# Forty-eight drains on TensorE between the loop and the tail of a decode kernel

## The chip, the core and the metric

The kernel runs on one core of a Trainium2 chip. Five engines of the core work side by side, each on its own stream of instructions: TensorE (PE in the profile, its weight loads PEld), VectorE (DVE), ScalarE (ACT), GpSimd (POOL) and SyncE (SP). They meet only at semaphores. Loads from the chip's main memory are issued here by SyncE and done by 16 DMA engines. An engine's sequencer reads the stream and hands products and vector operations on to the engine; drains, register steps and branches it does itself. The metric is the device time of one execution in microseconds (us); a profiled execution gives the trace and a page that sums it up.

## What is computed

One decode step of a block with attention and a gated feed-forward part side by side: batch 4, one token, width 512; 32 query heads over 8 key and value heads of 128; a window of the last 4096 of 16384 cached keys.

```python
xn = _layernorm(x, axis=-1)
return x + _A_ref(xn, ...) + _B_ref(xn, ...)

def _A_ref(x, k_cache, v_cache, wq, wo):
    q = (x @ wq)                                   # 32 heads of 128
    k = k_cache[:, :, Sk - W:, :]; v = v_cache[:, :, Sk - W:, :]
    scores = einsum("bhqd,bhkd->bhqk", q, k) * (Dh ** -0.5)
    p = softmax(scores, axis=-1)
    return einsum("bhqk,bhkd->bhqd", p, v) @ wo

def _B_ref(x, w_gate, w_up, w_down):
    return (silu(x @ w_gate) * (x @ w_up)) @ w_down
```

## The kernel before

The keys and values of 4 batches and 8 heads are cut into 16 pieces, each with one head of two batches, 2 MB of keys and 2 MB of values. Both are double-buffered in SBUF (`KB`, `VB`). SyncE issues all loads in one hand-written order: the query weights, two pieces of keys, the gate and up weights, then keys and values in turn, at last the down weights, the values of the last piece in two halves and the output weights `WO` in four cuts (chunks 0 to 15, 16 to 25, 26 to 29, 30 and 31 of 32). A load of keys waits until TensorE has transposed the keys that lay in its buffer (L216), a load of values until the products with the old values are done (`s_pv`, L220); the last values wait for the sixteenth of these (L241), the `WO` cuts behind them on the queue for nothing of their own.

TensorE runs a loop of 8 passes (L425) with two pieces in each. For a piece it transposes the keys (L382) into PSUM, from where VectorE copies them to SBUF (L294), forms the scores (`scores`, L385), and one piece later the products with the values (`pv`, L405). The maxima for the softmax go around by VectorE: it takes the row maxima of the scores (`row_max`, L299), TensorE transposes them (`max_rows`, L396, L398), VectorE reduces them to one value for each of 8 rows and makes a small diagonal of them (L304 to L306), TensorE subtracts that from all scores by one product (`shift`, L400), and ScalarE takes the exponential (L263). Helper `mm` (L353, recorded as L354) issues all products but the transposes.

Behind the loop stands a tail without a loop, in this order on TensorE: `max_rows` of the last piece (L439), the second half of the products with the values of the last but one (L440), the last `shift` (L441), the products with the gate and the up weights (L443 to L449), the input for the residual (L451), the products with the last values (L452 to L454), with the down weights (L457), four transposes of the attention's result (L462), a product that sorts the heads (L468), and 64 output products with `WO` (L472 to L476), which wait at chunks 0, 16, 26 and 30 for the four cuts. VectorE has in the tail the last maxima, normalisations of the attention's result (`norm`, L308), the gate, two copies of the sorted result (`OB` L345, `OP` L347) and the copy of the sum to SBUF (L349), from where two transfers of 2 KB take it out.

Everything on an engine runs in the order in which it is written; there is no planner.

Of the kernel before, what the change touches and what calls it, by code (L numbers as in the profile page):

```python
# [10 lines left out]
def bass_parallel_sum__sliding_block_cached__swiglu_ffn__decode_kernel(  # L11
# [10 lines left out]
    out: bass.AP,  # L22
):
    B, _, D = A_x.shape
    _, HKV, Sk, Dh = A_k_cache.shape
    HQ = A_wq.shape[1] // Dh
    F = B_w_gate.shape[1]
# [143 lines left out]
    with nc.Block() as block:  # L171
# [180 lines left out]
        def _(eng):  # L352
            def mm(o, l, r, start=False, stop=True):  # L353
                return eng.matmul(o, l, r, start=start, stop=stop, skip_group_check=True)  # L354
# [18 lines left out]
            def mask(bank):  # L373
                return mm(ps_S[bank][:].rearrange("p (t c) -> p t c", c=C), mkr[:],
                          mkc[:].rearrange("j (o c) -> j o c", o=1).to_broadcast([2, NT, C]), start=True)

            def transposes(s, ev, b):
                for g in range(NG):
                    eng.wait_ge(s_ev, ev + g + 1)
                    for k in range(8):  # L380
                        a = b * KVN + s * HKN + 128 * (8 * g + k)
                        last = eng.transpose(kt_ps[g][:, k, :], KB[:, a:a + 128], ident[:])  # L382
                    last.then_inc(s_tr, 1)

            def scores(s, ev, b, q):  # L385
                if s == 0:
                    mask(b)
                eng.wait_ge(s_ev, ev + 2 * NG)
                for t in range(HT):
                    o = C * (s * HT + t)  # L390
                    n = min(WIDE, SN - o)
                    last = mm(ps_S[b][:, o:o + n], KT[:, s * HKN + 128 * t:s * HKN + 128 * (t + 1)], q(n))
                if s == 1:
                    last.then_inc(s_sc, 1)

            def max_rows(n):  # L396
                eng.wait_ge(s_rm, n)
                mm(mt_ps, RM[:], ident[:], start=True).then_inc(s_mt, 1)  # L398

            def shift(bank, n):  # L400
                eng.wait_ge(s_dg, n)
                mm(ps_S[bank][:].rearrange("p (t c) -> p t c", c=C), ones[0:C, :],
                   Dg[:].rearrange("j (o c) -> j o c", o=1).to_broadcast([C, NT, C])).then_inc(s_sh, 1)

            def pv(bank, s, n):  # L405
                p = bank * PS
                if s == 0:
                    eng.wait_ge(d_v[bank], n[0])
                    eng.wait_ge(s_p, n[1])
                    eng.wait_ge(s_nrm, n[1])  # L410
                    for j in range(SN // 128):
                        mm(den_ps, ones[:], P[:, p + 128 * j:p + 128 * (j + 1)], start=(j == 0))
                for t in range(HT):
                    a = bank * KVN + s * HKN + 128 * t
                    o = p + C * (s * HT + t)
                    last = mm(O_wide, VB[:, a:a + 128], P[:, o:o + WIDE], start=(s == 0 and t == 0))
                if s == 1:
                    last.then_inc(s_pv, 1)
# [6 lines left out]
            with eng.Fori(0, ND // 2) as r:  # L425
                for b in range(2):
                    n = 2 * r + (b + 1)
                    ev = 4 * NG * r + 2 * NG * b
                    q = lambda w, b=b: QF[:, ds(r * (2 * WIDE) + b * WIDE, w)]
                    eng.wait_ge(d_k[b], r * 16 + 16)  # L430
                    transposes(0, ev, b)
                    max_rows(n)
                    pv(b, 1, n)
                    scores(0, ev, b, q)
                    shift(1 - b, n)
                    transposes(1, ev + NG, b)
                    pv(1 - b, 0, (r * 16 + 16, n))
                    scores(1, ev + NG, b, q)
            max_rows(ND + 1)  # L439
            pv(0, 1, ND + 1)  # L440
            shift(1, ND + 1)  # L441
# [64 lines left out]
```

## Time and profile before

| | us |
|---|---|
| median of 3 runs | 197.38 |
| lowest and highest run | 197.1, 198.93 |
| the profiled execution, its time | 196.99 |
| the profiled execution, its span | 195.2 |
| VectorE busy, share of the span | 59% |
| TensorE busy, share of the span | 82% |

The span goes from the first to the last recorded instruction; what lies around it, 1.8 us in the profiled execution, is start and end of the program. A line of the timeline has the start in us, the duration, the engine, the line of the kernel, the operation, the tile written and those read, and how many neighbours were merged; brackets hold the idle time ahead of it and who ended it. Engine names with a q (PEldq, SPq) are that engine's sequencer. The DMA engines are busy nearly all the way:

```profile
GB/s 216 430 430 433 435 423 428 425 433 433 430 437 430 430 433 430 430 437 430 433 430 433 430 430 433 430 430 430 430 433 430 430 430 433 430 431 417 442 404 64
```

Each number is the rate in one of 40 equal slices of the span.

### The profile page before, as it was taken

To read this page: it belongs to the slowest core of one execution; us is meant where nothing else is said; L and a number is where in the kernel's file an instruction comes from. 1 tells how busy PE (TensorE), PEld (TensorE's weight loads), DVE (VectorE), ACT (ScalarE), POOL (GpSimd) and SP (SyncE) were. 2 spreads that over 40 slices of the span, in tenths; PEclk is the share of its full clock that TensorE was granted. 3 is DMA by queue.
4 is the path that set the end of the run, shared out by engine and by line. 5 is a ranking of instruction groups with operands and counts; after the bars stand their busy time and mean duration, and the time that the engine had idled before them with its cause. 6 is when DMAs were issued, how large, how long until landed. Compare 5 with 4: busy or idle time off the path is not lost.

```text
span 195.2 us, 7741 instructions
## 1 busy us (share of the span) xinstructions
PE 160.9 (82%) x3458; PEld 139.5 (71%) x3458; DVE 114.8 (59%) x250; ACT 16.6 (9%) x26; POOL 10.3 (5%) x23
## 2 busy tenths in 40 slices
PE   0127999379898989898989898989898989898954
PEld 0113898368887888788878887878787878786742
DVE  1004777337676767676767676767676767675610
ACT  6600101001010101010101010101010101010100
POOL 8930000000000000000000000000000000000000
PEclk9999999879999999999999999999999999999999
DMA  6999999999999999999999999999999999999991
GB/s 216 430 430 433 435 423 428 425 433 433 430 437 430 430 433 430 430 437 430 433 430 433 430 430 433 430 430 430 430 433 430 430 430 433 430 431 417 442 404 64
DMA packets 5934, 81.10 MB, mean 416 GB/s; under 512 B 668, under 2 KB 680, under 8 KB 936
## 3 DMA queue, kind: packets, MB, share of 16 engines
q1 hardware_dynamic: 5912, 81.01, 97.5%
q8 instruction: 5, 0.08, 0.1%
q10 hardware_dynamic: 16, 0.01, 0.0%
q14 instruction: 1, 0.01, 0.0%
HBM read 81.01 MB, written 0.00 MB: 415 GB/s over the span
## 4 chain that ended last, share of the span: by engine, by line
DMA 63%; PE 32%; issue 1%; DVE 1%; SPq 1%; DVEq 0%
DMA kbuf<-in_A_k_cache_dram 48%; PE ps_kt L382 16%; DMA wo_sb<-in_A_wo_dram 9%; PE ps_s L354 8%; DMA wq_sb<-in_A_wq_dram 6%; PE ps_o L354 5%; PE ps_kt L354 2%; PE ps_acc L354 2%; DVE kT L294 1%; SPq L225 1%; DVE kT L282 0%; SPq L229 0%; DVE y_sb L349 0%; DVE qz L285 0%; DVEq L293 0%
## 5 line engine op out<-in xcount | busy, mean ns | idle before, releaser
L294 DVE COPY kT<-ps_kt 128x1024 bf16<-128x1024 bf16 x128 | 79.5, 684 | 25.3 <-PE ps_kt L382 25.3
L382 PE MATMUL ps_kt<-ident,kbuf 128*128 128x128 bf16 x1024 | 62.8, 219 | 10.6 <-DMA kbuf<-in_A_k_cache_dram 10.6
L382 PEld LDWEIGHTS ps_kt<-ident,kbuf 128*128 128x128 bf16 x1024 | 57.3, 98 | 15.8 <-issue 15.7
L354 PE MATMUL ps_o<-p,vbuf 128*128 128x64 bf16 x1120 | 39.0, 194 | 0.0
L354 PEld LDWEIGHTS ps_s<-qz,kT 128*128 128x128 bf16 x1024 | 32.1, 99 | 6.7 <-issue 3.6
L354 PEld LDWEIGHTS ps_o<-p,vbuf 128*128 128x128 bf16 x1120 | 35.8, 99 | 1.1
L354 PE MATMUL ps_s<-qz,kT 128*128 x1024 | 35.3, 193 | 1.2
L299 DVE TENSOR_REDUCE rm<-ps_s 128x8 bf16<-128x512 f32 x17 | 11.8, 692 | 23.5 <-PE ps_s L354 23.5
L263 ACT ACTIVATE p<-ps_s 128x512 bf16<-128x512 f32 x17 | 10.1, 597 | 162.4 <-PE ps_s L354 162.4
L354 PE MATMUL ps_o<-p,ones 128*128 128x128 bf16 (+1 forms) x69 | 6.9, 220 | 4.4 <-DMA vbuf<-in_A_v_cache_dram 3.0
L354 PEld LDWEIGHTS ps_o<-p,ones 128*128 128x128 bf16 x69 | 4.5, 98 | 5.5 <-DMA vbuf<-in_A_v_cache_dram 3.2
L354 PE MATMUL ps_kt<-wq_sb,xnT 128*32 128x512 bf16 x32 | 3.6, 629 | 5.6 <-DMA wq_sb<-in_A_wq_dram 5.6
L354 PE MATMUL ps_s<-dg,ones 8*128 8x512 bf16 x17 | 6.5, 385 | 0.0
L354 PE MATMUL ps_s<-mkc,mkr 2*128 2x512 bf16 x17 | 6.5, 385 | 0.0
L359 PE MATMUL ps_acc<-i,xn 4*128 4x4 f32 x4 | 0.6, 254 | 7.1 <-ACT xn L260 7.1
L354 PEld LDWEIGHTS ps_kt<-wq_sb,xnT 128*32 128x32 bf16 x32 | 1.2, 137 | 7.2 <-issue 7.2
L282 DVE STREAM_TRANSPOSE kT<-ps_kt 128x512 f32<-128x512 f32 x2 | 1.4, 716 | 8.3 <-PE ps_kt L354 8.3
L354 PE MATMUL ps_acc<-wo_sb,oP 128*4 128x256 bf16 x64 | 4.1, 272 | 1.8 <-DMA wo_sb<-in_A_wo_dram 1.8
L359 PEld LDWEIGHTS ps_acc<-i,xn 4*128 4x128 f32 x4 | 0.6, 207 | 7.1 <-issue 7.1
L310 DVE TENSOR_REDUCE den<-ps_o 128x8 f32<-128x128 f32 x18 | 4.9, 274 | 1.0 <-PE ps_o L354 1.0
L207 POOL MEMSET vbuf<- 128x6144 f32 x1 | 5.2, 5222 | 0.0
L354 PEld LDWEIGHTS ps_acc<-wo_sb,oP 128*4 128x4 bf16 x64 | 2.5, 84 | 3.3 <-DMA wo_sb<-in_A_wo_dram 1.9
(65 smaller groups left out, 48.0 us busy)
## 6 DMA issues: line engine op xcount, KB each, us to landing
kbuf<-in_A_k_cache_dram SPq DMA_DIRECT2D x16, 2048.0 KB, 12.6
vbuf<-in_A_v_cache_dram SPq DMA_DIRECT2D x15, 2048.0 KB, 11.3
wq_sb<-in_A_wq_dram SPq DMA_DIRECT2D x1, 4096.0 KB, 12.4
vbuf<-in_A_v_cache_dram SPq DMA_DIRECT2D x2, 1024.0 KB, 9.2
wo_sb<-in_A_wo_dram SPq DMA_DIRECT2D x1, 2048.0 KB, 14.4
wg_sb<-in_B_w_gate_dram SPq DMA_DIRECT2D x1, 1792.0 KB, 25.8
wu_sb<-in_B_w_up_dram SPq DMA_DIRECT2D x1, 1792.0 KB, 29.4
wd_sb<-in_B_w_down_dram SPq DMA_DIRECT2D x1, 1792.0 KB, 15.0
```

What stands on the lines that cost most here:

```text
L207: eng.memset(VB[:, HKN:].bitcast(FP32), 0.0)
L225: eng.dma_start(VB[:, a:a + HKN], kv_ap(A_v_cache, d)[:, :, h * HKN:(h + 1) * HKN]).then_inc(done, 16)
L263: eng.activation(P[:, d % 2 * PS:d % 2 * PS + SN], ps_S[d % 2][:], ACT.Exp, scale=SCALE).then_inc(s_p, 1)
L282: eng.transpose(qT[:, 512 * n:512 * n + 512], ps_kt[n][:])
L294: eng.tensor_copy(KT[:, u * HKN + 1024 * g:u * HKN + 1024 * (g + 1)], kt_ps[g].rearrange("p a b -> p (a b)")).then_inc(s_ev, 1)
L299: eng.tensor_reduce(RM[:], ps_S[bank][:].rearrange("p (t c) -> p c t", c=C), AX.X, ALU.max).then_inc(s_rm, 1)
L310: eng.tensor_reduce(den[:], den_ps.rearrange("p (t c) -> p c t", c=C), AX.X, ALU.add)
L354: return eng.matmul(o, l, r, start=start, stop=stop, skip_group_check=True)
L359: last = eng.transpose(xT_ps[:, c * B:(c + 1) * B], xn[:].rearrange("b (p c) -> b c p", c=NC)[:, c, :], I4[:])
L382: last = eng.transpose(kt_ps[g][:, k, :], KB[:, a:a + 128], ident[:])
```

## The change

Behind the loop and ahead of `max_rows(ND + 1)` TensorE gets 48 drain instructions. A drain is an instruction of the sequencer: it goes on when the engine's own work before it is done. They carry no semaphore, neither a wait nor a step. Nothing else differs; on the other four engines the programs are the same.

```diff
                     pv(1 - b, 0, (r * 16 + 16, n))
                     scores(1, ev + NG, b, q)
+
+            for _ in range(48):
+                eng.drain()
             max_rows(ND + 1)
             pv(0, 1, ND + 1)
             shift(1, ND + 1)
```

## The prediction

> **What bounds the kernel now.** I read the page's summary first, then the chain of waits in order of time, then the timeline behind the loop, and last single sequencer rows and stretches of the granted clock. The page's span and the last steps of the chain:
>
> ```profile
> span 195.2 us, 7741 instructions
> DMA 63%; PE 32%; issue 1%; DVE 1%; SPq 1%; DVEq 0%
> ...
> 170.88 1.05 PE ps_o L354 x32
> 171.95 0.54 SPq L225
> ...
> 173.83 16.82 DMA wo_sb<-in_A_wo_dram
> 190.64 0.04 issue
> 190.69 2.23 PE ps_acc L354 x32
> 192.92 0.03 issue
> 192.95 0.43 DVE y_sb L349
> ```
>
> The chain leaves TensorE at 171.95 us, inside the last pass of the loop, when the product that frees a V buffer lets SyncE issue its last loads. From there to 190.64 it is transfers. TensorE returns only for the second half of the output product, whose weights have just landed. So everything that TensorE does between 172 and 190 us, and the place of the change with it, lies beside the chain. The question is by how much. The timeline of that stretch (start, duration; in brackets the idle time before it and who ended it):
>
> ```profile
> 173.18 2.02 SPq L229 DMA_DIRECT2D wo_sb<-in_A_wo_dram  x4
> ...
> 176.73 1.06 PE L354 MATMUL ps_s<-qz,kT 128*128 x32
> 177.83 0.69 DVE L299 TENSOR_REDUCE rm<-ps_s 128x8 bf16<-128x512 f32 x1 [1.15 <-PE ps_s L354]
> ...
> 178.57 0.22 PE L354 MATMUL ps_acc<-ident,rm 128*8 128x128 bf16 x1 [0.78 <-DVE rm L299]
> ...
> 178.72 1.11 PE L354 MATMUL ps_o<-p,vbuf 128*128 128x64 bf16 x32
> ...
> 179.76 0.39 PE L354 MATMUL ps_s<-dg,ones 8*128 8x512 bf16 x1
> ...
> 180.08 0.94 PE L354 MATMUL ps_kt<-wg_sb,xnT 128*32 128x448 bf16 x16
> ...
> 182.17 2.03 PE L354 MATMUL ps_o<-p,vbuf 128*128 128x64 bf16 x64
> ...
> 184.13 1.69 PE L354 MATMUL ps_acc<-wd_sb,guT 128*4 128x256 bf16 x28
> ...
> 186.08 0.41 DVE L345 COPY oB<-ps_kt 32x512 bf16<-32x512 bf16 x1 [1.03 <-PE ps_kt L462]
> 186.54 0.22 PEld L354 LDWEIGHTS ps_kt<-oB,rep 32*128 32x128 bf16 x4 [0.68 <-DVE oB L345]
> ...
> 186.98 0.44 DVE L347 CAST oP<-ps_kt 128x128 bf16<-128x128 f32 x1 [0.49 <-PE ps_kt L354]
> 187.65 1.65 PEld L354 LDWEIGHTS ps_acc<-wo_sb,oP 128*4 128x4 bf16 x32 [0.89 <-DVE oP L347]
> 187.68 1.91 PE L354 MATMUL ps_acc<-wo_sb,oP 128*4 128x256 bf16 x32 [0.74 <-DMA wo_sb<-in_A_wo_dram]
> ...
> 192.52 0.09 PEld L354 LDWEIGHTS ps_acc<-wo_sb,oP 128*4 128x4 bf16 x4 [0.28 <-DMA wo_sb<-in_A_wo_dram]
> ```
>
> Three things are to be seen. TensorE stands idle for 0.78 us just where the drains go, waiting for VectorE's row maxima. From 178.57 on its products follow one another without a wait on a transfer, and the two hand-overs to VectorE at 186 us depend on them: a delay at 178.57 passes whole to 187.42, where `OP` is ready (186.98 + 0.44). At the output product it meets the slack. A hand-over from VectorE took 0.05 (186.08 + 0.41 to 186.54), so TensorE could have begun near 187.47 and began at 187.65, on a transfer: 0.18 us. The 32 products took 1.91, of which the last one's own time is some 0.27; that is (1.91 − 0.27)/31 = 0.053 each. Sixty of them would be done with at 187.68 + 60 × 0.053 = 190.86, and the last four begin at 192.52 on a transfer: 1.66 us. Together a delay of about **1.8 us is free**; beyond it each microsecond shows.
>
> **The change, step by step.** It removes and moves nothing. It adds 48 instructions for TensorE's sequencer. Behind them on TensorE stand the transposing product of L398 and all of the tail; VectorE's `shift` waits for that product and ScalarE's last exponential for the shift. SyncE is not held: its four `WO` issues begin at 173.18 and take 2.02, and nothing behind the loop frees a buffer for it. So no transfer moves, and with the last weights at 192.52 the end can't come earlier: a gain is excluded but for scatter.
>
> *The first drain* waits for the last score product. What that costs, and what a drain takes when nothing runs:
>
> ```profile
> L491 PEldq DRAIN  x1: 8/8/8, 0.3 to 0.3; - x1
> L171 PEldq DRAIN  x1: 432/432/432, 192.5 to 192.5; - x1
> L425 PEldq ALU_OP  x1: 32/32/32, 177.2 to 177.2; - x1
> L425 PEldq COMPARE_BRANCH  x1: 76/76/76, 177.3 to 177.3; - x1
> ```
>
> The drain at the kernel's end began at 192.5 and took 432 ns, to about 192.95, where the last product had ended (192.92 in the chain). So a drain waits for TensorE to run empty, and adds little more. The last scores end at 176.73 + 1.06 = 177.79; VectorE starts on them at 177.83. I let the first drain end at 177.84, and it costs nothing by itself.
>
> *The other 47* find TensorE empty. The drain at the start took 8 ns. What the sequencer needs between two of its own instructions has to come from others: the counter step and the branch of L425 stand next to each other in the program. Asked for in stretches of 10 ns, the first begins in 177.16 to 177.17 and the second in 177.26 to 177.27, so 98 ns apart with some 5 ns either way. Of these the first executes 32, and 66 pass between. A drain then costs about 8 + 64 = 72 ns, an estimate from these rows. The bounds: not under 8 ns, execution alone; not much over 98 ns, the whole distance, if a drain costs the sequencer what the counter step does. I take 72, since both parts are rows of TensorE's own sequencer. 47 × 0.072 = 3.38, so the last ends at 177.84 + 3.38 = 181.22, and the product begins with a hand-over of 0.03 (192.92 to 192.95) at 181.25 in place of 178.57: **a delay of 2.7 us**, less the slack of 1.8: 0.9 us at the end. The bounds by the same sum: 8 ns gives 47 × 0.008 = 0.38, done before the maxima are, and nothing; 98 ns gives 4.61, a delay of 3.9 and 2.1 at the end.
>
> The Trainium skill, "VectorE: DVE Perf Modes", section "The DRAIN you can't avoid", speaks of boilerplate drains of about 12 ns on all engines; by that the whole row would be 48 × 12 ns = 0.58 us, under the idle 0.78, and the change free. Its "Perfetto Trace Analysis", section "Sequencer-only Instruction (DRAIN, etc)", says that such a record holds execution alone, fetch and decode lying ahead of it; the 66 ns above agree.
>
> *The clock.* The drains leave TensorE without a product from 177.79 to 181.25, 3.46 us. What an idle stretch did to the clock, by stretches as long as the one at half clock (PE busy, PEld, DVE, ACT, POOL, granted clock, DMA), and what the half clock did to two groups:
>
> ```profile
> 34.55:37.96 3.41, 0.46 (x12) 0.46 (x13) 1.10 (x2) 0.00 (x0) 0.00 (x0) 1.00 1.01 425
> 37.96:41.37 3.41, 3.03 (x62) 2.94 (x58) 0.34 (x1) 0.00 (x0) 0.00 (x0) 0.50 0.99 418
> 184.73:188.14 3.41, 2.16 (x38) 1.58 (x36) 1.09 (x4) 0.00 (x0) 0.00 (x0) 1.00 0.97 414
> 191.56:194.97 3.41, 1.34 (x20) 0.44 (x14) 0.43 (x1) 0.00 (x0) 0.00 (x0) 1.00 0.04 13
> ...
> 194.97:195.17 0.20, 0.00 (x0) 0.00 (x0) 0.00 (x0) 0.00 (x0) 0.00 (x0) 0.51 0.00 0
> ...
> 37.50 0.40 PE L354 MATMUL ps_o<-p,ones 128*128 128x128 bf16 x4 [3.03 <-DMA vbuf<-in_A_v_cache_dram]
> 37.73 1.71 PE L354 MATMUL ps_o<-p,vbuf 128*128 128x64 bf16 x32
> ```
>
> An idle time of 3.03 us left one stretch of 3.41 with 0.46 us of product, and the next ran at half clock. So did what followed the stretch with 1.34. The one with 2.16 did not do it. With stretches of that length laid over an idle 3.46 us at any phase, one of the two that share it holds at least 1.73 of idle, so at most 1.68 of product; in four of five phases it holds 1.34 or less. The half clock is then likely, and its stretch lies 2.1 to 3.4 us deep in the products that follow. The 32 products of 64 columns took 1.71 against 1.11: at that ratio 3.41 us at half clock do the work of 2.2, and 1.2 are lost; products that wait for the columns alone would lose half, 1.7. With 2.1 us so lost at the least ratio it is 0.7. I take **1.3 us**, all beyond the slack, since the 1.8 is used up.
>
> The sum: 2.7 − 1.8 + 1.3 = **2.2 us**. The profiled execution took 196.99 beside its span of 195.2, which makes 199.2; the median of the three runs was 197.38 (197.1 to 198.93), which makes 199.6. I put it between, at 199.4, from a base of 197.2.
>
> **The rivals.** *The clock stays.* The drains cost 72 ns, the delay is 2.7, and 0.9 shows: 198.1. For it: a stretch between 1.34 and 2.16 of product is not in the trace, and one phase in five falls there. Against: both low stretches were followed by the half clock. The Trainium skill, "TensorE: Matmul & The Clock Gate", Part 1, wants at least one idle window of about 3.4 us before the clock drops, in windows that run free of the kernel; by it the gap of 3.46 would almost never hold a whole one, and the result would be this 198.1. The stretch with 0.46 us of product speaks against that rule here.
>
> *The drains are cheap, and it is not slower.* The place is the wait for the maxima and the slack at the output product; the price is the drain's, and it decides at (1.8 + 178.57 − 0.03 − 177.84)/47 = 0.053 us. Under 53 ns a drain, nothing shows but what the clock adds; at 16 ns they end within the idle 0.78. For it: the record of 8 ns. Against: the 66 ns between two neighbours on the same sequencer. Time: 197.2.
>
> *The drains are dearer.* At 98 ns each the delay is 3.9, of which 2.1 show, and with the clock's 1.4 it is 3.5: 200.7. A fetch of the longer program would fall here too. The queue of instructions is this row of the page:
>
> ```profile
> q8 instruction: 5, 0.08, 0.1%
> ```
>
> 0.1% of 16 × 195.2 us is 3.1 us for five, 0.6 each at most if one were exposed. Against it: no row of the sequencer but the branch shows more than 98 ns.
>
> That the change doesn't do what it says: drains could be dropped when the program is built. The built program has the 48 in a row ahead of the product, so I give this nothing beyond the cheap case.
>
> **How the numbers follow.** Cheap 0.20, clock stays 0.13, forecast 0.52, dearer 0.15. The forecast's own range is 198.7 (clock at 0.7, a base of 197.0) to 200.2. For 8 in 10 the range reaches down to the cheap case, as its price is an end of the unknown cost, and up to the dearer one: 197.0 to 201.0. A change of under 1%, 1.97 us, can't be told from none here. The forecast of 2.2 lies just past it: some seven tenths of its chance fall beyond, 0.36, the dearer case nearly whole, 0.15, and a little of the second, 0.01: slower 0.52. Faster 0.01 for scatter, the rest, 0.47, within.
>
> **What would show it.** In the changed profile: 48 drains on TensorE's sequencer, the first ending near 177.8 us, the others about 72 ns apart with 8 ns of execution; the transposing product near 181.2 with an idle time of about 3.4; half the granted clock in a stretch of 3.41 us that begins between 179.9 and 182.7; `WO` issued at 173.2 and landed as before; the wait ahead of the last four output products gone. The chain of waits should then run over TensorE's tail and not over `WO`. Wrong it would be if the drains stood much closer or wider, if the clock stayed whole, or if the chain still ended on the `WO` transfer.

## The result and the profile after

The changed kernel took 200.02 us, the median of 6 runs (199.47 to 200.67), against 197.29 of 6 runs before: a ratio of 1.0121 with a 95% interval of 1.0083 to 1.016, so 1.6 to 3.2 us slower, 2.4 at the middle. The profiled execution took 199.47 with a span of 197.7, 2.5 us more than the one before. It was the shortest of the six.

The rows of the new line, first all drains, then those that begin after 178.0 us:

```profile
L441 PEldq DRAIN  x48: 7/8/435, 177.5 to 181.2; - x48
...
L441 PEldq DRAIN  x47: 7/8/13, 178.0 to 181.2; - x47
```

One drain waited 435 ns, from 177.5 to the end of the scores; the other 47 took about 8 ns each and their starts stand (181.2 − 178.0)/46 = 0.070 us apart. What they did to the tail shows in the timeline of the changed kernel:

```profile
176.83 1.06 PE L354 MATMUL ps_s<-qz,kT 128*128 x32
177.93 0.69 DVE L299 TENSOR_REDUCE rm<-ps_s 128x8 bf16<-128x512 f32 x1 [1.16 <-PE ps_s L354]
...
181.30 0.22 PE L354 MATMUL ps_acc<-ident,rm 128*8 128x128 bf16 x1 [3.41 <-issue]
...
181.45 1.11 PE L354 MATMUL ps_o<-p,vbuf 128*128 128x64 bf16 x32
...
182.49 0.60 PE L354 MATMUL ps_s<-dg,ones 8*128 8x512 bf16 x1
...
183.02 1.68 PE L354 MATMUL ps_kt<-wg_sb,xnT 128*32 128x448 bf16 x16
...
184.49 1.63 PE L354 MATMUL ps_kt<-wu_sb,xnT 128*32 128x448 bf16 x16
...
191.32 0.44 DVE L347 CAST oP<-ps_kt 128x128 bf16<-128x128 f32 x1 [0.49 <-PE ps_kt L354]
191.82 3.66 PE L354 MATMUL ps_acc<-wo_sb,oP 128*4 128x256 bf16 x64 [0.53 <-DVE oP L347]
195.52 0.42 DVE L349 CAST y_sb<-ps_acc 128x256 bf16<-128x256 f32 x1 [3.75 <-PE ps_acc L354]
```

The maxima were ready at 178.62, and the product that transposes them began at 181.30; the wait ahead of it is put down to "issue", for which the profile shows no releaser, and no longer to VectorE; it is the time in which the drains stand. The product was 2.73 us later than before (178.57), of which 0.10 came out of the loop with the scores (176.83 against 176.73). `OP` was ready at 191.76, 4.34 later (187.42): 1.61 us were lost on the way, and the gate and up products show where, with 1.68 and 1.63 us. The gate products had taken 0.94 and the up products 0.93; the rest of the 1.61 lies in the last `shift`, with 0.60 for 0.39. All 64 output products then ran without a wait, and the last copy began 2.57 late (192.95).

The stretches of the granted clock in the changed kernel (length, PE, PEld, DVE, ACT and POOL busy, clock, DMA):

```profile
175.67:179.08 3.41, 2.14 (x67) 1.93 (x64) 1.79 (x3) 0.00 (x0) 0.00 (x0) 1.00 0.97 409
179.08:182.49 3.41, 1.19 (x33) 1.08 (x34) 0.50 (x2) 0.00 (x0) 0.00 (x0) 1.00 1.07 454
182.49:185.91 3.42, 3.42 (x36) 1.18 (x33) 1.31 (x4) 0.85 (x2) 0.00 (x0) 0.50 1.00 425
185.91:189.32 3.41, 3.41 (x90) 2.96 (x88) 2.25 (x8) 0.00 (x0) 0.00 (x0) 1.00 0.96 404
```

A stretch with 1.19 us of product was followed by one at half clock, and that one lay on the gate and up products. The chain of waits of the changed kernel ends so:

```profile
177.93 0.70 DVE rm L299
178.63 2.67 issue
...
183.09 3.02 PE ps_kt L354 x21
186.34 2.20 PE ps_o L354 x68
188.54 1.62 PE ps_acc L354 x28
...
191.82 3.68 PE ps_acc L354 x64
```

Before, the chain lay on the `WO` transfer from 173.83 to 190.64. Now it goes from the scores over the drains and TensorE's tail; no transfer is left in it behind the loop.

### The profile page after: what moved, and what is told of

Its sections match the earlier page's. It is cut to its first block, busy times and chain, and to the rows that moved or that the text cites. A ratio compares the mean times of both kernels' runs of the same rounds, so it can differ in the third digit from the quotient of the medians.

```text
span 197.7 us, 7789 instructions
## 1 busy us (share of the span) xinstructions
PE 163.9 (83%) x3458; PEld 141.5 (72%) x3458; DVE 115.5 (58%) x250; ACT 16.6 (8%) x26; POOL 10.3 (5%) x23
## 4 chain that ended last, share of the span: by engine, by line
DMA 52%; PE 41%; issue 3%; DVE 3%; DVEq 0%
DMA kbuf<-in_A_k_cache_dram 45%; PE ps_kt L382 18%; PE ps_s L354 9%; PE ps_o L354 7%; DMA wq_sb<-in_A_wq_dram 6%; PE ps_acc L354 4%; PE ps_kt L354 4%; DVE kT L294 1%; DVE kT L282 0%; DVE rm L299 0%; DVE oP L347 0%; DVE y_sb L349 0%; DVE oB L345 0%; DVE qz L285 0%; PE ps_kt L465 0%
## 5 line engine op out<-in xcount | busy, mean ns | idle before, releaser
L382 PE MATMUL ps_kt<-ident,kbuf 128*128 128x128 bf16 x1024 | 65.7, 224 | 11.0 <-DMA kbuf<-in_A_k_cache_dram 10.7
L382 PEld LDWEIGHTS ps_kt<-ident,kbuf 128*128 128x128 bf16 x1024 | 60.1, 101 | 16.4 <-issue 16.4
L354 PE MATMUL ps_o<-p,vbuf 128*128 128x64 bf16 x1120 | 38.4, 193 | 0.0
L354 PEld LDWEIGHTS ps_s<-qz,kT 128*128 128x128 bf16 x1024 | 31.4, 98 | 6.6 <-issue 3.6
L354 PEld LDWEIGHTS ps_o<-p,vbuf 128*128 128x128 bf16 x1120 | 35.2, 98 | 1.2
L354 PE MATMUL ps_s<-qz,kT 128*128 x1024 | 34.7, 192 | 1.2
L354 PE MATMUL ps_acc<-ident,rm 128*8 128x128 bf16 x17 | 3.8, 222 | 3.4 <-issue 3.4
L304 DVE TENSOR_REDUCE m<-ps_acc 8x1 f32<-8x128 f32 x17 | 4.6, 270 | 2.9 <-PE ps_acc L354 2.9
```

The source lines that it names most:

```text
L304: eng.tensor_reduce(m8[:], mt_ps, AX.X, ALU.max)
```

## The experiments

The theory: the drains hold TensorE's sequencer for 70 ns each, TensorE then stands idle long enough for one stretch of half clock, and of both together 1.8 us are free. Against it stood that the drains cost by their number, wherever they stand; that the clock has no part; and that a drain itself does harm beyond the idle time.

**Half the drains.**

```diff
-            for _ in range(48):
+            for _ in range(24):
                 eng.drain()
```

> 24 drains in place of 48. Own theory (a drain costs TensorE's sequencer some 70 ns, the idle time ahead of the product covers the first 0.8 us and the wait for WO another 1.8): the last drain ends 1.6 us after the first, the transposing product is 0.9 to 1.0 us late, OP too, and the end not at all: within 0.3 us of the kernel before. TensorE is idle for 1.7 us; should the clock drop for one stretch, 0.5 us at most show. Rival, every drain shows at the end: half of the 2.4 to 2.7 us of the 48, so 1.2 to 1.4 us slower.

Measured: a ratio of 1.0007 (0.9989 to 1.0024), median 197.46 of 10 runs against 197.2. From its timeline:

```profile
179.67 0.22 PE L354 MATMUL ps_acc<-ident,rm 128*8 128x128 bf16 x1 [1.74 <-issue]
...
188.40 0.44 DVE L347 CAST oP<-ps_kt 128x128 bf16<-128x128 f32 x1 [0.49 <-PE ps_kt L354]
...
192.78 0.09 PEld L354 LDWEIGHTS ps_acc<-wo_sb,oP 128*4 128x4 bf16 x4 [0.29 <-DMA wo_sb<-in_A_wo_dram]
```

The product was 1.10 late and `OP` 1.42, and yet the last four output products waited for the last cut of `WO`, as before. The end was not late beyond the noise, so the delay is there and covered. The 0.3 us between the two lie in a gap among the products with the down weights, which I did not follow up.

**Twice the drains.**

```diff
-            for _ in range(48):
+            for _ in range(96):
                 eng.drain()
```

> 96 drains in place of 48. Own theory: no cover is left, so the 48 more cost 48 x 0.070 = 3.3 us in full; the transposing product comes near 184.6 us, and the end is 5.6 us behind the kernel before (4.7 to 6.4, by how long the half clock lasts). Rival, drains in a row get cheaper or dearer, or a longer program has to be fetched: the distance of the drains in the trace leaves 0.07 us and the end leaves that range.

Measured: 1.0308 (1.027 to 1.0346), so 6.1 us slower (5.3 to 6.8); median 203.7 of 4 runs. The drains in its profile:

```profile
L441 PEldq DRAIN  x96: 7/8/435, 178.3 to 185.7; - x96
```

Behind the first they stand (185.7 − 178.3 − 0.44)/95 = 0.073 us apart, against 0.070 with 48; one gap, of which more at the end, makes up most of the difference. So a drain in the longer row is hardly dearer, and the rival finds little here. That the first 24 cost nothing and the last 48 some 3.7 us agrees with a fixed cover and a price for each beyond it. In the profiled execution, the longest of the four, the half clock lasted from 181.52 to 191.76, and 2.64 us were lost between the product and `OP`.

**The same delay with TensorE at work.**

```diff
-            for _ in range(48):
-                eng.drain()
+            for _ in range(16):
+                mm(ps_kt[3][:], ones[:], KT[:, 0:512], start=True)
```

> No drains; in their place 16 products of 512 columns into a PSUM bank that is free there, so that TensorE is held about as long but works. They add work whose result nothing reads. Own theory: the transposing product is late by some 2.6 us as with the drains, but the granted clock stays whole in the tail, and the end is late by that delay less 1.8, so 0.8 us (0.4 to 1.2). Rival, the clock has no part in the loss and the delay alone makes it: 2.2 to 2.7 us slower, as with the drains.

Measured: 1.0023 (1.0006 to 1.004), 0.1 to 0.8 us slower; median 197.85 of 10 runs. From its timeline:

```profile
177.77 3.61 PE L354 MATMUL ps_kt<-kT,ones 128*128 128x512 bf16 x16
181.31 0.22 PE L354 MATMUL ps_acc<-ident,rm 128*8 128x128 bf16 x1
...
182.82 0.94 PE L354 MATMUL ps_kt<-wg_sb,xnT 128*32 128x448 bf16 x16
...
189.72 0.44 DVE L347 CAST oP<-ps_kt 128x128 bf16<-128x128 f32 x1 [0.49 <-PE ps_kt L354]
...
193.65 0.09 PEld L354 LDWEIGHTS ps_acc<-wo_sb,oP 128*4 128x4 bf16 x4 [0.29 <-DMA wo_sb<-in_A_wo_dram]
```

The transposing product began at 181.31, with the drains at 181.30. But the gate products took 0.94 as before the change, and `OP` was 2.74 late, no more than the product itself. The rival without the clock falls: the same delay is worth 0.5 us without the half clock and 2.4 with it, by the two ratios. That it is 0.5 and not the delay less the slack, 0.9, has a likely reason in the last line. In this execution the last cut of `WO` landed 18.7 us after its issue, against 17.7 in the profile before, and the last four output products waited for it once more. The end is the later of TensorE's tail and that transfer; where the transfer is late by itself, less of the delay shows. The executions of the kernel before reach from 196.95 to 198.18, these only from 197.76 to 198.23, which agrees, but the landing is known of the profiled ones alone.

**The drains at another place.**

```diff
-            for _ in range(48):
-                eng.drain()
             max_rows(ND + 1)
             pv(0, 1, ND + 1)
             shift(1, ND + 1)
+            for _ in range(48):
+                eng.drain()
```

> The 48 drains moved two steps back, behind the last shift and ahead of the gate products, where TensorE has no idle time of 0.8 us. Own theory: the gate products begin 3.4 to 3.5 us late, where they were 2.9 late with the drains in their first place, the clock drops as it did there, and the end is 3.0 us behind the kernel before (2.4 to 3.4). Rival, the place doesn't matter as the drains cost the same everywhere: gate products 2.9 us late, end 2.4 to 2.7.

Measured: 1.0188 (1.015 to 1.0225), so 3.7 us slower (3.0 to 4.4); median 201.39 of 4 runs, more than I expected. The gate products began at 183.82, 3.74 later than before the change, where 48 drains ahead of the maxima made them 2.94 late: without the idle 0.78 as a cover the drains cost more, and the rival that the place doesn't matter falls. Its stretches tell of the rest:

```profile
179.51:182.92 3.41, 0.86 (x20) 0.51 (x16) 0.77 (x4) 0.60 (x1) 0.00 (x0) 1.00 1.07 452
182.92:186.33 3.41, 2.50 (x28) 1.17 (x32) 0.65 (x1) 0.09 (x1) 0.00 (x0) 0.50 0.98 417
186.33:189.75 3.42, 3.42 (x53) 2.59 (x46) 1.66 (x5) 0.16 (x1) 0.00 (x0) 0.50 0.96 405
```

The half clock lasted two stretches, not one, and `OP` was 6.46 late (193.88), so 2.72 us were lost behind the start of the gate products where I had counted on one stretch.

**Idle without drains.**

```diff
             eng.engine_nop().then_inc(d_v[1], 16)
+            eng.wait_ge(s_sc, ND + 1)
+            eng.memset(KB[:, 0:7860].bitcast(FP32), 0.0).then_inc(s_idle, 1)
...
-            for _ in range(48):
-                eng.drain()
+            eng.wait_ge(s_idle, 1)
             max_rows(ND + 1)
```

> No drains. GpSimd waits for the last scores and then clears 7860 columns of an idle key buffer, some 3.35 us by its 5.22 us for 6144 elements of fp32; the transposing product waits for that as well as for the maxima. Own theory: all that the drains do is to hold TensorE idle; the product comes near 181.3 us, one stretch of half clock follows, and the end is 2.4 to 2.9 us behind the kernel before, as with the 48 drains. Rival, drains cost something of their own beyond the idle time, by their number or by restarting an empty engine: then this is nearer to the 16 products, 0.5 to 1.0 us slower.

Measured: 1.0132 (1.0089 to 1.0174), so 2.6 us slower (1.8 to 3.4); median 200.39 of 4 runs. The wait, from the timeline:

```profile
181.36 0.27 PE L357 MATMUL ps_acc<-ident,rm 128*8 128x128 bf16 x1 [3.49 <-POOL kbuf L213]
```

The same idle time from another cause costs the same within the intervals, and the rival of 0.5 to 1.0 us falls. A price of the drains beyond the idle time is not to be seen; a small one would be lost in the interval. In this profile the half clock also lasted two stretches, and `OP` was ready at 192.90 (192.46 and 0.44), 5.48 late with the product 2.79 late.

**Half drains, half products.**

```diff
-            for _ in range(48):
+            for _ in range(24):
                 eng.drain()
+            for _ in range(8):
+                mm(ps_kt[3][:], ones[:], KT[:, 0:512], start=True)
```

> 24 drains and behind them 8 of the products of the third experiment, whose result nothing reads. Own theory: the transposing product comes near 181.3 us as with 48 drains, but TensorE is idle for only 1.7 us, as with the 24 drains alone, and the clock stays whole: 0.4 to 1.0 us slower, as with the 16 products. Rival, a delay with drains in it is dearer than the same delay without them, whatever the clock: half of the difference between 48 drains and 16 products remains, 1.5 us slower or more.

Measured: 1.0061 (1.0027 to 1.0095), so 1.2 us slower (0.5 to 1.9), median 198.12 of 10 runs. The ten fall into two groups: six from 197.75 to 198.3 with a mean granted clock of 0.991 or 1.0, four from 199.33 to 199.9 with 0.965 to 0.983. The profiled one is of the first group:

```profile
176.91:180.32 3.41, 1.70 (x35) 1.16 (x32) 0.69 (x1) 0.00 (x0) 0.00 (x0) 1.00 1.00 422
180.32:183.73 3.41, 3.41 (x59) 2.00 (x61) 1.16 (x5) 0.60 (x1) 0.00 (x0) 1.00 1.06 447
```

A stretch with 1.70 us of product left the clock whole; the transposing product began at 181.30, `OP` was ready at 190.15 (189.71 and 0.44), 2.73 late like the product, and the last copy began at 193.90, 0.95 late. So in this execution a delay with drains in it was no dearer, and the clock stayed. The interval of all ten is wide, reaches beyond what I expected and takes in the 1.5 us of the rival, so the ratio alone doesn't decide between the two. An idle time of 1.7 us may lie at the edge. That the four longer executions lost the clock just there is likely but not shown: no profile of one was taken, and a lower mean clock doesn't tell where it was lost (an execution of the kernel before with 0.974 took 197.11 us).

**Other instructions of the sequencer.** Two waits are packed into one instruction, so these are 30 instructions.

```diff
-            for _ in range(48):
-                eng.drain()
+            for _ in range(60):
+                eng.wait_ge(s_const, 2)
```

> No drains; in their place 30 instructions of TensorE's sequencer that wait for two semaphores which have long come, the last of them for the maxima. Own theory: the price is that of any instruction that the sequencer does itself, its execution (51 ns for such a wait in the profile of before) and some 60 ns to the next, so 0.11 us each and 3.4 us in all; they begin at 177.5 and don't wait for the last scores, the product comes near 180.9, and the end is 1.8 to 2.5 us behind the kernel before. Rival, the 60 ns belong to a drain, which asks the engine whether it is empty: the waits cost 0.05 us each, are done by 179.1, and nothing shows.

Measured: 1.0115 (1.0073 to 1.0156), so 2.3 us slower (1.4 to 3.1); median 199.53 of 4 runs. The sequencer's rows of the new line, 29 of the 30, as the last goes by the line of the maxima:

```profile
L441 PEldq EVENT_SEMAPHORE  x29: 51/51/51, 177.7 to 180.7; - x29
```

and the product in the timeline:

```profile
180.94 0.22 PE L354 MATMUL ps_acc<-ident,rm 128*8 128x128 bf16 x1 [2.85 <-issue]
```

Waits that have long passed stand (180.7 − 177.7)/28 = 0.107 us apart, with 51 ns of execution: 56 ns between two, with a drain 62 (70 − 8), and with the counter step of the prediction 66. The three kinds seen here pay much the same between two, and the rival that it belongs to the drain falls.

## Why the prediction was right

It gave 199.4 for a measured 200.02 and slower as the likeliest, and the steps can be set against what was measured in the profiled execution. That it came out as slower is in part luck: the forecast of 2.2 us lay barely past the 1.97 us below which it called a change none, with chances of 0.52 and 0.47, and the measured 1.6 to 3.2 us reaches below that bound too.

*The first drain* was to end at 177.84 and cost nothing. It ended at 177.94, with the whole tail 0.10 later out of the loop, so it is right, and those 0.10 are in this run's delays below.

*The other 47* were to cost 72 ns by the distance of two neighbours on the sequencer. They stood 70 ns apart. That one pair of neighbours gave so close a figure has some luck in it: between the pair 66 ns passed, and with drains 60 for most and 90 for some (the last section). The 8 ns of the records were not the price: what passes between two records was nearly all of it, and the passed waits show the same. The Trainium skill's 12 ns ("VectorE: DVE Perf Modes", "The DRAIN you can't avoid") were not the price here either. That the record holds execution alone is what the Trainium skill's "Perfetto Trace Analysis", "Sequencer-only Instruction (DRAIN, etc)", says, and the 8 ns beside the 70 agree.

*The delay* of the product was to be 2.7 and was 2.73; *the slack* 1.8, and it can be read in each profile in which the output products ran without a wait for `WO`, as the lateness of `OP` less that of the last copy:

| | product late | OP late | of it lost on the way | last copy late | slack |
|---|---|---|---|---|---|
| 48 drains | 2.73 | 4.34 | 1.61 | 2.57 | 1.77 |
| 24 drains and 8 products | 2.73 | 2.73 | 0.00 | 0.95 | 1.78 |
| idle without drains | 2.79 | 5.48 | 2.69 | 3.71 | 1.77 |
| 30 passed waits | 2.37 | 3.89 | 1.52 | 2.11 | 1.78 |
| 96 drains | 7.20 | 9.84 | 2.64 | 8.07 | 1.77 |
| 48 drains behind the shift | 3.74 (gate) | 6.46 | 2.72 | 4.68 | 1.78 |

All against the profile before (178.57, 187.42, 192.95; the moved drains by the start of the gate products, 180.08). Of the 7.20 with 96 drains, 0.91 came out of the loop (177.64 against 176.73). Not in the table are the 24 drains and the 16 products, whose last output products waited for `WO`; there the same difference is 1.17 and 1.62.

*The clock* is the term that was mis-sized, though the mechanism was right: I took 1.3 us between 0.7 and 1.7, and it cost 1.61. The 1.3 leaned towards products that lose half their speed or less; the stretch fell on the gate and up products, which took 1.68 us for 0.94. And I let the half clock last one stretch. It can last two, and costs 2.7 then; that some of the six runs had two would make the median, 2.73 over that of before, larger than the profiled difference of 2.5, but no profile of such a run of this kernel was taken. That 2.73 + 1.61 − 1.77 gives the 2.57 of the last copy is no test, as the last two terms are differences of the same four times; what tests the slack is that the way from `OP` to the last copy took 3.75 or 3.76 us in all six profiles of the table, against 5.53 before, where it waited for `WO`.

Some steps of the working were loose and changed little. It read 66 ns between the pair and added 64; with 66 a drain is 74 ns and the delay 2.8. The lower end of the forecast's own range, with 197.0, 0.9 and 0.7, is 198.6 and not 198.7, and the dearer rival took 1.4 for the clock where the forecast took 1.3. The sentence that no row of the sequencer but the branch shows more than 98 ns overlooked the drain of 432 ns, which it had shown, and a semaphore instruction of 111 (L410).

Of the rivals, *the clock stays* was nearly what the 16 products made true, 0.5 us where it gave 0.9, and in the profiled execution with 48 drains it did not happen. The Trainium skill's rule behind it ("TensorE: Matmul & The Clock Gate", Part 1: at least one idle window of about 3.4 us) does not hold here as worded: in the tail of the changed kernel no stretch was wholly idle, and one with 1.19 us of product sufficed. *The drains are cheap* fell with the 70 ns; the cover it counted on was real, as 24 drains showed. *The drains are dearer* did not come. What was to show a step wrong, `WO` as the end of the chain, was not there.

## What to carry to other kernels

Price an instruction that an engine's sequencer does itself by the distance to its neighbour, not by its record: on TensorE here 56 to 66 ns passed between two, with drains, passed waits and a counter step. Follow an added delay to the place where the tail meets a transfer and subtract the slack there. If the delay is idle time of TensorE, look at the granted clock as well: the same 2.7 us cost 0.5 us at the end with products in it and 2.4 without.

## What the runs showed that I had not expected

*The half clock can last.* At full clock a stretch with 1.70 us of product left it whole and one with 1.34 did not. At half clock a stretch with 2.50 us of product (the moved drains) was followed by another at half clock; so was this one of the idle run, while its next, busy throughout, ended it:

```profile
180.68:184.09 3.41, 2.73 (x38) 2.05 (x42) 0.99 (x4) 0.07 (x1) 0.62 (x1) 0.50 1.05 449
184.09:187.50 3.41, 3.41 (x36) 1.23 (x29) 1.18 (x3) 0.78 (x2) 0.00 (x0) 0.50 0.98 410
187.50:190.92 3.42, 3.42 (x92) 3.12 (x92) 1.96 (x8) 0.00 (x0) 0.00 (x0) 1.00 0.94 389
```

In the kernel before, 3.03 us of product had ended it. So by busy time between 2.73 and 3.03 us of 3.41 were needed to lift it, and between 1.34 and 1.70 to keep it. That isn't the same work, since a product is busy longer at half clock. The 38 products of the 2.73 us took from 178.57 to some 180.27 in the kernel before, 1.70 us at full clock (an estimate: the gate products began at 180.08, the up products 0.76 later, and 4 of the 16 gate products are among the 38). Whether it takes more work to lift the clock than to keep it stays open.

*Every sixteenth instruction is dearer.* Starts of drains in the trace of the changed kernel, in us:

```
178.480 178.548 178.616 178.715 178.783
179.603 179.671 179.740 179.838 179.906
180.726 180.795 180.863 180.961 181.030
```

The distance is 68 ns, and 98 after each sixteenth; the passed waits had 106 and 136 likewise. With the moved drains the two dearer ones had 136 and 126. With 96 drains, one drain began 230 ns after its forerunner, at the place of a sixteenth, and took 124, and the next began 185 ns after it. What makes either was not tried.
